# Loading and preparing the first chunk by halves of the heads, under a new fixed order

## The chip, the cores and the metric

The kernel runs on one core of one Trainium2 chip. Its time is the device time of one execution in microseconds (us). The engines are TensorE (PE, matrix products; PEld is its weight load), VectorE (DVE), ScalarE (ACT), GpSimd (POOL) and SyncE (SP), whose queue issues nearly all transfers. 16 DMA engines move the data.

## The reference

There are two stages. The first is a recurrence over 768 steps for 4 batches of 8 heads with head size 40. Each head has a 40x40 state:

```
y[t]  = r[t] @ state                                   (before the update)
Sa    = state @ a[t]
state = state * w[t] - outer(Sa, b[t]) + outer(v[t], k[t])     (w along the columns)
```

The second takes the rows of y (3072 tokens, 320 wide) through `relu(x @ w_in)**2 @ w_out`, with 2048 hidden columns. Inputs and output are 32-bit floats.

## The kernel before

**Chunks.** The recurrence is cut into 12 chunks of 64 steps. In a chunk all 32 heads are worked on together: 16 heads stand in the lower 64 rows of a tile, 16 in the upper. NP is 8, the heads of one batch; the two "halves" h0 and h1 of this text are the first and the second batch in each half of the rows.

**A chunk's preparation** (function `prep`). `ln` takes the logarithm of w on ACT (L453). `hi` is its 16-bit part (L374 where POOL does it) and `lo` the 16-bit remainder (L380 on DVE, L378 on POOL). PE sums both along the steps by a triangular matrix: `ci` by halves of the heads and `cf` for all heads turned. ACT takes exponentials of these sums: `ei` (L475, into iG), `ex` (L481, into Gin), `ef` (L497, into GT). `mulKB` multiplies k and b by iG, by halves; `castA`, `castR`, `castV` bring a, r and v to 16 bits. `TK`, `TA`, `TR` are transposes on PE, and `tK`, `tA`, `tR` take their results out of PSUM. `EN` is a triangle of products, masked by `mEN` (L578).

**The recurrence and its reading** (`rec`, `read`). `AS`, `EV`, `u0`, `NU`, `u1` solve for the chunk's updates, `SC`, `S` and `s` make the next state, `TS` turns it. `TV`, `CX`, `RS` and `Y` give the chunk's rows of y, `XT` turns these for the second stage.

**The second stage** (`ffn`). For each chunk four entries `F` (first 256 rows of w_in) and four `FL` (last 64 rows), `f` (relu, L802 on ACT), `q` (square: L810 POOL, L808 DVE, L812 ACT), and four `O`, the product with w_out; `o` copies it out, `st` stores it. In the last chunk the copy and the store are split in two parts `g0`, `g1`, with `o0`, `st1` on ACT, `o1` on DVE and `st0` on SP.

**The weights** are loaded once, between the first chunks: `lwl` (last rows of w_in), `lwi u0` to `u3` (quarters of w_in, 512 KB each), `lwo x0` to `x7` (pieces of w_out, 320 KB each). They pass through two staging places each, and are cast to 16 bits by `cwl`, `cwi` and `cwo`.

**Loads of the inputs** are `ldw`, `ldk`, `ldb`, `ldv`, `lda`, `ldr`, two DMAs each for one chunk. Two buffers stand for each input, so a load may be issued once the chunk two before it has been used.

**What sets the order.** Each piece of work is an entry ("ACT ln 0", "PE2 TK 0", where the figure is one of four PSUM places). The text ORDER lists all of them, and `issue` emits them in this sequence, so each engine works its entries off strictly in the order of the text. The text is written out in the kernel; it was made by a search outside it, which used the costs given with each entry. Because this order is fixed, the trace's instructions can be matched to the entries one by one on each engine.

On PE an entry works in one of four tilings, given as `mode`: "R" uses 64 rows by 128 columns (ci, cf, EN, CX, FL and all transposes), "Q" 64 by 64 (EV, NU), "C" 128 by 64 (AS, SC, S, RS, Y), "D" 128 by 128 (F, O). The profile writes these as 64*128, 64*64, 128*64 and 128*128.

Of the kernel before, what the change touches and what calls it, by code (L numbers as in the profile page):

```python
# [86 lines left out]
ORDER = """SP ldw 0; SP lda 0; SP ldb 0; SP ldk 0; ACT ln 0; SP ldw 1; POOL hi 0; POOL castA 0; DVE lo 0; PE0  # L87
TA 0; SP lda 1; PE1 ci 0 h0; PE2 ci 0 h1; ACT ex 0 h0 g1; PE3 cf 0; ACT ex 0 h1 g0; ACT ei 0 h1;
ACT ex 0 h1 g1; ACT ei 0 h0; SP ldv 0; ACT ef 0; DVE mulKB 0 h1; SP ldw 2; ACT ex 0 h0 g0; DVE
mulKB 0 h0; DVE tA 0 g0; PE2 TK 0; DVE tK 0; ACT ln 1; SP ldk 1; POOL hi 1; DVE tA 0 g1; PE3 EN 0  # L90
g0; POOL lo 1; DVE mEN 0 g0; PE1 EN 0 g1; DVE mEN 0 g1; SP ldb 1; PE2 ci 1 h1; POOL castV 0 g0;
ACT ei 1 h1; POOL castV 0 g1; ACT ex 1 h1 g1; ACT ex 1 h1 g0; POOL castA 1; PE0 EV 0; SP ldr 1;
PE3 cf 1; ACT u0 0; PE1 ci 1 h0; ACT ln 2; PE NU 0; ACT ex 1 h0 g1; PE2 TA 1; POOL hi 2; ACT ef 1;
SP lda 2; DVE lo 2; ACT u1 0 g0; DVE tA 1 g0; ACT ei 1 h0; SP ldv 1; PE3 S 0 g0; DVE tA 1 g1; ACT
ex 1 h0 g0; ACT u1 0 g1; PE1 ci 2 h0; SP ldr 0; ACT ex 2 h0 g1; PE S 0 g1; DVE mulKB 1 h0; PE2 TV
0; DVE mulKB 1 h1; ACT ei 2 h0; DVE s 0 q1; ACT tV 0; SP ldw 3; PE0 TK 1; DVE s 0 q0; SP ldk 2;
DVE tK 1; PE3 TS 0; ACT tS 0; PE2 EN 1 g1; PE0 cf 2; DVE mEN 1 g1; SP ldb 2; PE3 EN 1 g0; ACT ef
2; POOL castR 0; DVE mEN 1 g0; ACT ex 2 h0 g0; POOL castV 1 g1; ACT castA 2; PE2 TR 0; PE0 ci 2
h1; POOL castV 1 g0; ACT tR 0 g0; PE1 AS 1; SP lwl 0; ACT tR 0 g1; POOL castR 1; PE EV 1; ACT ln
3; PE3 CX 0 g0; PE2 CX 0 g1; ACT u0 1; POOL hi 3; DVE mCX 0 g0; ACT ex 2 h1 g1; PE NU 1; POOL lo  # L100
3; ACT ex 2 h1 g0; SP lwi 0 u0; ACT ei 2 h1; DVE mCX 0 g1; PE3 TR 1; ACT u1 1 g0; PE0 TA 2; ACT tR
1 g1; DVE tA 2 g1; PE2 Y 0; SP ldv 2; ACT tR 1 g0; ACT u1 1 g1; PE3 SC 1; DVE mulKB 2 h1; PE1 TV
1; SP ldr 2; PE S 1 g0; DVE tA 2 g0; ACT tV 1; PE S 1 g1; DVE y 0; DVE mulKB 2 h0; ACT cwl 0; DVE
yd 0; PE0 TK 2; DVE s 1 q0; PE1 ci 3 h1; POOL cwi 0 u0; SP lwi 0 u1; PE2 CX 1 g0; DVE tK 2; ACT ei
3 h1; ACT ex 3 h1 g0; ACT ex 3 h1 g1; SP lwo 0 x1; DVE s 1 q1; PE0 cf 3; PE1 EN 2 g0; DVE mCX 1
g0; ACT ef 3; PE3 TS 1; POOL castV 2 g1; SP lwo 0 x0; ACT tS 1; DVE mEN 2 g0; PE0 EN 2 g1; POOL
castR 2; PE2 AS 2; SP ldb 3; POOL castV 2 g0; DVE mEN 2 g1; PE3 ci 3 h0; PE1 XT 0; ACT ex 3 h0 g0;
POOL cwi 0 u1; ACT ei 3 h0; DVE xt 0; PE EV 2; ACT ex 3 h0 g1; SP lwi 0 u3; PE0 CX 1 g1; ACT u0 2;
PE1 FL 0 u1; DVE mCX 1 g1; PE NU 2; SP lda 3; PE3 RS 1; ACT u1 2 g0; PE0 SC 2; PE Y 1; DVE u1 2
g1; SP ldk 3; PE F 0 u1; DVE y 1; SP lwi 0 u2; DVE yd 1; PE S 2 g0; ACT f 0 u1; PE S 2 g1; PE2 TR  # L110
2; DVE s 2 q0; PE3 FL 0 u3; ACT tR 2 g1; POOL cwi 0 u3; DVE s 2 q1; ACT tR 2 g0; SP ldw 4; DVE q 0
u1; POOL castA 3; PE F 0 u3; POOL cwo 0 x0; PE1 TV 2; ACT f 0 u3; DVE cwo 0 x1; PE2 XT 1; PE0 TS
2; SP lwo 0 x2; ACT tV 2; PE3 F 0 u0; DVE tS 2; POOL mulKB 3 h0; DVE xt 1; PE0 TA 3; PE FL 0 u0;
SP lwo 0 x3; DVE tA 3 g1; PE2 FL 1 u3; ACT f 0 u0; PE1 CX 2 g0; POOL cwi 0 u2; DVE tA 3 g0; PE F 1
u3; SP ldv 3; DVE mulKB 3 h1; PE3 F 1 u2; ACT f 1 u3; DVE mCX 2 g0; SP ldr 3; PE0 TK 3; ACT ln 4;
PE FL 1 u2; PE2 FL 1 u1; DVE tK 3; PE1 CX 2 g1; ACT f 1 u2; POOL hi 4; PE F 1 u1; POOL cwo 0 x2;
DVE mCX 2 g1; PE3 F 1 u0; POOL lo 4; ACT cwo 0 x3; PE0 EN 3 g0; ACT f 1 u1; SP lwo 0 x5; PE FL 1
u0; DVE mEN 3 g0; PE1 F 0 u2; ACT f 1 u0; SP lwo 0 x4; PE FL 0 u2; DVE q 0 u0; PE2 EN 3 g1; POOL
castV 3 g0; PE0 cf 4; ACT f 0 u2; DVE mEN 3 g1; PE3 ci 4 h0; SP ldw 5; POOL castV 3 g1; ACT ef 4;
PE1 RS 2; DVE q 0 u2; PE Y 2; ACT ei 4 h0; PE2 AS 3; DVE yd 2; PE EV 3; DVE cwo 0 x5; ACT ex 4 h0  # L120
g1; DVE y 2; PE0 O 0 u0; SP lwo 0 x7; ACT u0 3; POOL cwo 0 x4; DVE q 1 u0; ACT ex 4 h0 g0; POOL
castR 3; ACT q 0 u3; PE1 ci 4 h1; SP lwo 0 x6; PE NU 3; ACT ex 4 h1 g1; PE3 TR 3; ACT u1 3 g0; SP
ldk 4; PE O 0 u1; DVE tR 3 g1; ACT ex 4 h1 g0; DVE u1 3 g1; ACT ei 4 h1; PE O 0 u2; POOL cwo 0 x7;
SP ldb 4; ACT tR 3 g0; ACT ln 5; PE1 XT 2; DVE cwo 0 x6; PE2 TV 3; SP lda 4; POOL hi 5; DVE xt 2;
PE3 SC 3; ACT tV 3; PE S 3 g0; POOL lo 5; PE S 3 g1; PE O 0 u3; DVE s 3 q1; SP ldv 4; DVE s 3 q0;
POOL q 1 u1; PE1 ci 5 h0; ACT o 0; PE2 CX 3 g0; SP ldk 5; PE3 cf 5; ACT ex 5 h0 g0; DVE mCX 3 g0;
# [831 lines left out]
```

## Time and profile before

| | us |
|---|---|
| median of 3 runs | 255.05 |
| lowest, highest run | 252.43, 256.12 |
| profiled execution | 251.61 |
| its span, first to last instruction | 249.8 |
| PE busy in the span | 219.0 (88%) |
| DVE busy | 181.7 (73%) |
| ACT busy | 172.7 (69%) |
| POOL busy | 117.9 (47%) |
| DMA, share of 16 engines, loads and stores of SP | 66.1% |

Busy times are averages over stretches that differ. A row of a group or of the timeline names the line of the kernel, the engine, the operation, and what it writes from what; in square brackets stands the idle time of the engine just before it and what ended that. The line is often that of a helper (L384 is every matmul, L388 every transpose, L374 every cast on POOL), so the tiles tell which entry it is: `pb<-XT,WIN` is F, `pb<-XT,WLAST` is FL, `pb<-WOUT,G` is O, `WIN<-G` is cwi, and `G<-in_moe_w_in_dram` is lwi or lwl.

### The profile page before, as it was taken

What the parts mean: (1) busy time and instruction counts of PE and PEld (TensorE: products, weight loads), DVE (VectorE), ACT (ScalarE), POOL (GpSimd) and SP (SyncE); (2) the same over time, 40 slices, a digit from 0 to 9 for tenths busy, and PEclk for the clock granted to TensorE, in tenths of its full rate; (3) what the DMA queues carried; (4) which work ended last, traced back from release to release, by engine and by line L of the source; (5) the groups of instructions that cost most, each with busy time, mean ns of one, the idle gap of its engine ahead of it and who ended that gap; (6) DMA issues with size and microseconds to landing.
All of it is one profiled execution on the core that took longest, in us unless ns stands there. A gap on an engine that the chain in (4) does not pass through costs nothing.

```text
span 249.8 us, 12572 instructions
## 1 busy us (share of the span) xinstructions
PE 219.0 (88%) x5752; PEld 170.7 (68%) x5752; DVE 181.7 (73%) x227; ACT 172.7 (69%) x231; POOL 117.9 (47%) x119
## 2 busy tenths in 40 slices
PE   0458877777999999999999999999999999999991
PEld 0336765565777777787778778877777777877770
DVE  7585869768787897867868958788778899746221
ACT  2548897756897866788659788895798351863930
POOL 4261341534636587473487870625369930452000
PEclk9999997999999999999999999999999999999998
DMA  6999889999988987878877888976480020201121
GB/s 132 170 150 211 156 172 204 230 228 187 188 213 157 158 209 150 172 167 163 165 178 134 142 136 209 158 169 127 110 140 5 4 58 5 55 3 29 26 55 52
DMA packets 114091, 33.58 MB, mean 134 GB/s; under 512 B 101238, under 2 KB 113014, under 8 KB 114038
## 3 DMA queue, kind: packets, MB, share of 16 engines
q1 hardware_dynamic: 113894, 32.62, 66.1%
q8 instruction: 45, 0.74, 1.3%
q10 hardware_dynamic: 144, 0.16, 0.2%
q14 instruction: 8, 0.07, 0.1%
HBM read 28.84 MB, written 3.93 MB: 131 GB/s over the span
## 4 chain that ended last, share of the span: by engine, by line
PE 61%; ACT 14%; issue 7%; DVE 7%; POOL 6%; DMA 3%; SPq 1%; POOLq 0%; ACTq 0%
PE pb L384 52%; PE pb L388 8%; ACT Gin L481 2%; POOL G L810 2%; ACT iG L475 2%; DMA raw_a<-in_a_dram 2%; DMA raw_w<-in_w_dram 2%; ACT G L802 2%; DVE EN L578 2%; ACT GT L497 2%; ACT VUT L370 1%; DVE KBT L365 1%; DVE AR L365 1%; ACT AR L370 1%; ACT osb L370 1%
## 5 line engine op out<-in xcount | busy, mean ns | idle before, releaser
L802 ACT ACTIVATE G<-pb 128x1024 bf16<-128x1024 f32 x44 | 44.6, 1021 | 19.5 <-PE pb L384 17.4
L384 PE MATMUL pb<-WOUT,G 128*128 128x320 bf16 x384 | 57.3, 300 | 0.0
L810 POOL TENSOR_TENSOR G<-G 128x1024 bf16<-128x1024 bf16 x21 | 41.1, 1966 | 23.3 <-ACT G L802 23.2
L384 PE MATMUL pb<-XT,WIN 128*128 128x256 bf16 x384 | 48.5, 273 | 1.3 <-POOL WIN L374 1.3
L384 PEld LDWEIGHTS <-G 128*128 128x128 bf16 x384 | 35.3, 98 | 14.8 <-issue 1.4
L384 PEld LDWEIGHTS <-WIN 128*128 128x128 bf16 x384 | 34.9, 98 | 8.9 <-issue 2.5
L578 DVE TENSOR_TENSOR CX<-pb,MSKI 128x1024 bf16<-128x1024 f32 x24 | 29.1, 1221 | 7.3 <-PE pb L384 7.0
L578 DVE TENSOR_TENSOR EN<-pb,MSK 128x1024 bf16<-128x1024 f32 x24 | 28.9, 1221 | 6.7 <-PE pb L384 6.4
L481 ACT ACTIVATE Gin<-pb 64x320 f32<-64x320 f32 x48 | 20.6, 429 | 10.3 <-PE pb L384 9.7
L374 POOL CAST VU<-raw_v 64x640 bf16<-64x640 f32 x24 | 17.8, 742 | 12.7 <-DMA raw_v<-in_v_dram 12.1
L670 DVE TENSOR_TENSOR STb<-pb,GT 64x640 bf16<-64x640 f32 x22 | 18.0, 820 | 3.6 <-PE pb L384 3.1
L370 ACT ACTIVATE osb<-pb 128x640 f32<-128x640 f32 (+1 forms) x13 | 8.3, 640 | 17.4 <-PE pb L384 17.0
L374 POOL CAST hi<-lnW 128x640 bf16<-128x640 f32 x12 | 9.2, 767 | 21.9 <-ACT lnW L453 16.9
L475 ACT ACTIVATE iG<-pb 128x640 f32<-128x640 f32 x24 | 16.7, 696 | 3.8 <-PE pb L384 3.6
L384 PEld LDWEIGHTS <-EN 64*64 64x64 bf16 x768 | 15.0, 113 | 6.2 <-issue 3.6
L380 DVE TENSOR_TENSOR KB<-raw_kb,iG 128x640 bf16<-128x640 f32 x16 | 14.4, 914 | 6.7 <-DMA raw_kb<-in_b_dram 4.1
L553 DVE TENSOR_TENSOR AR<-pb,GT 128x512 bf16<-128x512 bf16 x24 | 15.8, 684 | 2.2 <-PE pb L388 2.0
L384 PE MATMUL pb<-XT,WLAST 64*128 64x256 bf16 x192 | 17.2, 271 | 0.1
L808 DVE TENSOR_TENSOR G<-G 128x1024 bf16<-128x1024 bf16 x13 | 11.0, 850 | 8.4 <-ACT G L802 8.4
L378 POOL TENSOR_TENSOR KB<-raw_kb,iG 128x640 bf16<-128x640 f32 x8 | 12.6, 1583 | 8.3 <-ACT iG L475 4.1
L370 ACT ACTIVATE VUT<-pb 128x2048 bf16<-128x2048 bf16 x8 | 15.0, 1873 | 2.2 <-PE pb L388 2.2
L365 DVE COPY KBT<-pb 128x2048 bf16<-128x2048 bf16 x11 | 13.4, 1220 | 3.5 <-PE pb L388 3.5
(82 smaller groups left out, 414.9 us busy)
## 6 DMA issues: line engine op xcount, KB each, us to landing
raw_w<-in_w_dram SPq DMA_DIRECT2D x24, 160.0 KB
raw_a<-in_a_dram SPq DMA_DIRECT2D x24, 160.0 KB
raw_kb<-in_b_dram SPq DMA_DIRECT2D x24, 160.0 KB
raw_kb<-in_k_dram SPq DMA_DIRECT2D x24, 160.0 KB
raw_v<-in_v_dram SPq DMA_DIRECT2D x24, 160.0 KB
raw_r<-in_r_dram SPq DMA_DIRECT2D x22, 160.0 KB
out_dram<-osb SPq DMA_DIRECT2D x22, 160.0 KB
osb<-in_moe_w_out_dram SPq DMA_DIRECT2D x8, 320.0 KB
```

The lines of the kernel that those rows point to most:

```text
L365: lambda: nc.vector.tensor_copy(out=o_(), in_=i_())))
L370: alts.append(("ACT", c_act(n), lambda: nc.scalar.activation(out=o_(), in_=i_(), func=ACTF.Copy, scale=1.0 if scale is None else scale)))
L374: lambda: nc.gpsimd.tensor_copy(out=o_(), in_=i_())))
L384: return lambda: nc.tensor.matmul(out=o_(), lhsT=l_(), rhs=r_(), start=start, stop=stop, skip_group_check=True)
L388: return lambda: nc.tensor.transpose(out=o_(), in_=i_(), identity=IDb[rows(g), :])
L475: ew(f"ei {c} h{jh}", [("ACT", c_act(2 * n), lambda hb=hb, jh=jh: nc.scalar.activation(out=iG[0][:].rearrange("p (g j) e -> p g (j e)", g= ...
L481: nc.scalar.activation(out=Gin[c % NGI][rows(g), NP * jh:NP * jh + NP, :].rearrange("p j e -> p (j e)"), in_=slot(hb, FP32)[rows(g), g, 0: ...
L553: ew(f"tA {c} g{g}", [("DVE", c_dve(512), lambda g=g: nc.vector.tensor_tensor(out=steps(AR[q2][:, 0, g]), in0=turned(ha, g), in1=steps(GT[ ...
L578: evac(f"m{nm} {c} g{g}", lambda s, n: [("DVE", c_dve(n), lambda: nc.vector.tensor_tensor(out=dst[q2][:, g, s].rearrange("p q i t -> p (q ...
L670: ew(f"s {c} q{q}", [("DVE", c_dve(2 * n), lambda q=q: nc.vector.tensor_tensor(out=STb[q2][rows(q), :, q, 0:D], in0=slot(hs, FP32)[rows(q) ...
L802: ("ACT", c_act(1024), lambda gb=gb, hf=hf: nc.scalar.activation(out=gb, in_=slot(hf, FP32)[:], func=ACTF.Relu)),
L810: ("POOL", 1900, lambda gv=gv: nc.gpsimd.tensor_tensor(out=gv, in0=gv, in1=gv, op=ALU.mult)),
```

## The change

For chunk 0 alone, three loads and three steps of the preparation become two entries each, one for each half of the heads:

- `ldw 0`, `ldk 0`, `ldb 0` become `h0` and `h1`, of two DMAs each; a DMA now brings one batch (8 heads, 80 KB) instead of two.
- `ln 0`, `hi 0`, `lo 0` become `h0` and `h1`, on 320 columns instead of 640.
- `ci 0 h0` waits for `hi` and `lo` of its own half alone, and `mulKB 0 h0` for its own half of k and b. `cf 0` waits for both halves.

For the other chunks nothing is split. The text ORDER is replaced as a whole: for all 12 chunks the sequence on each engine, the engine of many elementwise entries and the PSUM place of many products are others than before.

```
+    def parts(c):
+        return [(f" h{j}", (j,)) for j in range(2)] if c == 0 else [("", (0, 1))]
...
+        def quarter(x, g, j):
+            return x[2 * g + j, :, t0, :].rearrange("h t e -> t h e")
...
+            def go(x=x, ring=ring, js=(0, 1)):
+                for g in range(2):
+                    if len(js) == 2:
+                        nc.sync.dma_start(out=ring[c % len(ring)][rows(g)], in_=half(x, g))
+                    else:
+                        nc.sync.dma_start(out=ring[c % len(ring)][rows(g), NP * js[0]:NP * js[0] + NP],
+                                          in_=quarter(x, g, js[0]))
+            for sfx, js in parts(c):
+                plan.add(f"ld{nm} {c}{sfx}", [("SP", 1200 * len(js))],
+                         ("ew", {"SP": lambda go=go, js=js: go(js=js)}),
+                         writes=[("raw", nm, c % len(ring), j) for j in js])
...
-        ew(f"ln {c}", [("ACT", c_act(640), lambda: nc.scalar.activation(
-            out=lw[:], in_=raw_w[c % NW][:], func=ACTF.Ln))],
-           reads=[("raw", "w", c % NW)], writes=[("lnW",)])
...
+        for sfx, js in parts(c):
+            j0, nj = NP * js[0], NP * len(js)
+            def js_(x, j0=j0, nj=nj):
+                return x[:, j0:j0 + nj]
+            ew(f"ln {c}{sfx}", [("ACT", c_act(D * nj), lambda js_=js_: nc.scalar.activation(
+                out=js_(lw), in_=js_(raw_w[c % NW]), func=ACTF.Ln))],
+               reads=[("raw", "w", c % NW, j) for j in js], writes=[("lnW", j) for j in js])
...
-            pe(f"ci {c} h{jh}", "R", n, ms, reads=[("hi",), ("lo",)], writes=[hb], alloc=[hb])
+            pe(f"ci {c} h{jh}", "R", n, ms, reads=[("hi", jh), ("lo", jh)], writes=[hb], alloc=[hb])
```

The loads of SP, in order, up to the last piece of w_out:

```
before: ldw 0; lda 0; ldb 0; ldk 0; ldw 1; lda 1; ldv 0; ldw 2; ldk 1; ldb 1; ldr 1; lda 2; ldv 1;
  ldr 0; ldw 3; ldk 2; ldb 2; lwl 0; lwi 0 u0; ldv 2; ldr 2; lwi 0 u1; lwo 0 x1; lwo 0 x0; ldb 3;
  lwi 0 u3; lda 3; ldk 3; lwi 0 u2; ldw 4; lwo 0 x2; lwo 0 x3; ldv 3; ldr 3; lwo 0 x5; lwo 0 x4;
  ldw 5; lwo 0 x7; lwo 0 x6
after: ldw 0 h1; ldw 0 h0; ldk 0 h0; ldk 0 h1; ldb 0 h0; ldb 0 h1; ldw 1; lda 0; ldv 0; ldw 2;
  lda 1; ldk 1; ldb 1; ldr 0; lwi 0 u0; ldr 1; ldv 1; lda 2; ldk 2; ldb 2; ldw 3; ldr 2; lwl 0;
  lda 3; ldv 2; lwo 0 x1; lwi 0 u1; ldb 3; lwo 0 x3; lwi 0 u3; ldk 3; lwo 0 x0; lwi 0 u2; ldw 4;
  ldr 3; lwo 0 x2; lda 4; ldv 3; lwo 0 x5; lwo 0 x4; ldw 5; lda 5; lwo 0 x7; lwo 0 x6
```

The first entries of the other engines after the change, and the last of ACT:

```
ACT   ln 0 h1; ln 0 h0; ei 0 h1; ef 0; ex 0 h1 g0; ei 0 h0; ex 0 h0 g1; ex 0 h0 g0; ln 1; ...
POOL  hi 0 h1; hi 0 h0; lo 0 h1; lo 0 h0; mulKB 0 h1; castA 0; lo 1; castV 0 g1; castV 0 g0; ...
DVE   mulKB 0 h0; hi 1; tK 0; tA 0 g0; tA 0 g1; mEN 0 g0; mEN 0 g1; tA 1 g1; ...
PE    ci 0 h1; ci 0 h0; cf 0; TK 0; TA 0; EN 0 g0; cf 1; EN 0 g1; ci 1 h0; ci 1 h1; EV 0; ...
ACT   ... o 10; o0 11 g0; st1 11 g0; o0 11 g1; st1 11 g1     (before: o0 g0; o0 g1; st1 g0; st1 g1)
```

More of the change, by code (lines that the diff above doesn't have):

```diff
@@ L98 @@
[L98 to L103, printed above, removed]
@@ L110 @@
[L110 to L115, printed above, removed]
@@ L122 @@
[L122 to L126, printed above, removed]
-PE0 FL 2 u1; ACT ef 5; PE F 2 u1; DVE mulKB 4 h0; ACT ex 5 h0 g1; PE2 F 2 u2; ACT f 2 u1; SP ldb
```

279 lines of the change are left out of this document (151 added, 128 removed).

## The prediction

> **What bounds the kernel now.** I read the engines' busy times by stretches first, then the timeline at the places where TensorE (PE) stands, then the queue that issues the loads (SPq). Columns of the first view: stretch, PE busy (matmuls), weight loads, DVE, ACT, POOL, granted clock, DMA share, GB/s.
>
> ```profile
> 0.00:20.00 20.00, 7.14 (x180) 5.46 (x182) 13.71 (x28) 8.66 (x14) 8.11 (x22) 1.00 1.02 152
> 20.00:40.00 20.00, 16.61 (x532) 13.45 (x528) 14.88 (x19) 17.48 (x27) 5.65 (x7) 0.92 0.92 190
> 40.00:60.00 20.00, 14.62 (x514) 11.89 (x515) 15.20 (x20) 14.07 (x18) 8.10 (x9) 1.00 1.01 206
> 60.00:80.00 20.00, 18.09 (x459) 13.56 (x458) 15.04 (x20) 15.93 (x23) 11.29 (x13) 1.00 0.88 193
> 80.00:160.00 80.00, 78.52 (x2130) 61.30 (x2125) 63.12 (x74) 61.85 (x85) 49.17 (x44) 1.00 0.83 164
> 160.00:240.00 80.00, 79.59 (x1937) 62.09 (x1934) 57.83 (x67) 53.40 (x67) 35.62 (x26) 1.00 0.30 63
> ```
>
> Two regimes show. Up to 60 us the DMA engines are full (shares 1.02, 0.92, 1.01) and PE is busy 38.4 of 60 us. From 80 us PE is busy 158.1 of 160 us and nothing else matters. The seam is one load, the third quarter of the first weight matrix:
>
> ```profile
> 60.62 1.15 POOL L374 CAST WIN<-G 128x1024 bf16<-128x1024 f32 x1 [0.58 <-DMA G<-in_moe_w_in_dram]
> 61.82 0.39 PE L384 MATMUL pb<-XT,WIN 128*128 128x256 bf16 x2 [1.35 <-POOL WIN L374]
> ```
>
> POOL waits for the DMA, casts, and PE waits 1.35 us for the cast (entry F 1 u2 of the order). Past this point PE hardly waits. So the time is: when F 1 u2 may start, plus PE's own work behind it, plus its waits, plus the tail.
>
> PE's work I take from starts of neighbouring entries. This stretch of its timeline shows how:
>
> ```profile
> 84.06 1.92 PE L384 MATMUL pb<-XT,WIN 128*128 128x256 bf16 x16
> 85.92 0.39 PE L384 MATMUL pb<-XT,WLAST 64*128 64x256 bf16 x4
> 86.15 0.30 PE L384 MATMUL pb<-hi,UTI 64*128 64x320 bf16 x2
> 86.28 0.30 PE L384 MATMUL pb<-lo,UTI 64*128 64x320 bf16 x2
> 86.42 0.40 PE L384 MATMUL pb<-AR,VUT 64*128 64x64 bf16 x16
> 86.75 1.26 PE L384 MATMUL pb<-WOUT,G 128*128 128x320 bf16 x8
> ```
>
> An FL entry (rows 64*128, x4) takes 0.23 us from its start to that of another 64*128 entry (85.92 to 86.15). A CX entry (x16) takes 86.75 - 86.42 = 0.33 where a 128*128 entry follows; the median CX followed by its own kind takes 0.24. The step between tilings thus costs 0.09 us. By the same difference O costs 1.10 and 1.19, F 0.88 and 0.97, FL 0.23 and 0.32, S 0.25 and 0.34: 0.095 us a step. Medians of the unswitched entries in us: F 0.88, O 1.10, FL 0.23, ci 0.28, cf, TK, TV and TS 0.47, EN, CX, TA and TR 0.24, EV and NU 0.52, Y 0.51, RS, SC and AS 0.30, S 0.25, XT 0.18. Summed from F 1 u2 on, the old order has 163.4 us of work and 150 tiling steps (14.2 us): 177.6. From 61.8 this gives 239.4; the last matmul ends at 244.4, so 5.0 us are waits, in small pieces.
>
> **The change, part by part.**
>
> **1. The halves at the start: 0 at the seam.** Each of w, k, b of chunk 0 becomes two entries of two DMAs: 12 issues where 6 were, and the load of a moves behind all of them and the next w.
>
> ```profile
> 0.79 1.46 SPq L400 DMA_DIRECT2D raw_w<-in_w_dram  x2
> 2.30 1.31 SPq L421 DMA_DIRECT2D raw_a<-in_a_dram  x2
> 3.65 1.33 SPq L407 DMA_DIRECT2D raw_kb<-in_b_dram  x2
> 5.83 0.74 ACT L453 ACTIVATE lnW<-raw_w 128x640 f32<-128x640 f32 x1 [3.76 <-DMA raw_w<-in_w_dram]
> ```
>
> An issue takes 0.65 to 0.73 us. Two issues end at 2.25 and the logarithm starts at 5.83, 3.6 us later; the first half cannot save more than its share of the data (160 KB at 152 GB/s: 1.1 us), so ln 0 h1 starts near 4.6. The second half's issues end near 3.4, so its logarithm gains nothing (about 5.7). A half Ln costs some 0.43 (the 64x320 rows of L481), a half cast some 0.4 and a half subtraction on POOL 0.7 (half of 1.45). POOL's queue is hi h1, hi h0, lo h1, lo h0: from 6.1 it ends near 8.0, where DVE's whole lo ended at 8.76. That gains 0.8 us for ci and cf. But it is spent at once: b's last half is issued by 8.7 and lands near 10.5, a is issued 10.0 to 11.3 and lands near 13.2, and POOL has the half product mulKB (1.58) ahead of the cast of a (0.73). TA 0, done at 8.75 before, comes at 14; hi 1 (0.5 to 0.7) now stands before tK 0 on DVE. I get EN 0 at 16.0, against 15.34. Bounds of this edit for the first products: 1 us earlier to 1 us later. The DMA stream, not this chain, sets the seam at 60 us and hides it, so it enters as 0; without that cover it would be the 0.7 us of EN 0.
>
> **2. The stream starts slower: +1.0.** Twelve issues at 0.66 take 7.9 us; their data (80 KB each at 152 GB/s: 0.54 us) take 6.5. So the issuing queue holds the stream back by 1.4, and a full stream doesn't catch up. Bounds: 0 (later queueing absorbs it) to 2. The Trainium skill ("DMA: Bandwidth & Descriptors", Issuing engines are not separate DMA queues) says that the time on the sequencer to initiate a DMA is usually small relative to the DMA itself; by it this term would be 0 and the forecast 1.0 lower. The rows here, 0.66 to issue against 0.54 to move, speak against it for pieces of this size.
>
> **3. The new order of loads: +1.3.** Counted to the load that gates F 1 u2 (lwi 0 u2), both orders hold w, a, k, b of four chunks, v and r of three, the last rows of the first matrix and its four quarters; the new one has three pieces of the second matrix ahead of it instead of two. A piece is 320 KB; at 206 GB/s 1.6 us, and its packets near 61 us ran 1.3. Bounds 0 to 1.6. The cast goes from POOL to DVE; the cast's 640 columns took 0.67 on DVE and 0.72 on POOL, so nothing is gained. F 1 u2 starts at 61.8 + 1.0 + 1.3 = 64.1.
>
> **4. PE's work behind it: +2.0.** The new order holds 164.1 us there and 163 tiling steps (15.5): 179.6 against 177.6. Before it PE has room, so what was moved there costs nothing. In all the new order makes 194 steps, the old 181; the products are the same.
>
> **5. Waits: -1.2.** The other engines gain 2.3 us of lead at the seam; I let a half of that come off the 5.0 us. Bounds -3 to +3: the last piece of the second matrix (lwo 0 x6) now has two more loads of a ahead of it, lands later by 2 to 4 us than its 74.9, and O 0 u3, which started at 78.0, would come near 64.1 + 15.2 = 79.3, so it can wait a microsecond.
>
> **6. Tail: +0.6.** At the end ACT's queue had both copies, then both stores; now a store stands before the second copy.
>
> ```profile
> 245.14 0.30 ACT L370 ACTIVATE osb<-pb 128x160 f32<-128x160 f32 x1 [0.39 <-DVE osb L365]
> 245.15 0.99 ACTq L854 DMA_DIRECT2D out_dram<-osb  x2
> 245.48 0.33 DVE L365 COPY osb<-pb 128x160 f32<-128x160 f32 x1 [0.37 <-ACT osb L370]
> ```
>
> The store's issue on ACT takes 0.3 to 0.63 us; the copy that went beside it, DVE's behind it, and the last stores wait for it. Bounds 0.3 to 0.65.
>
> **Sum**: +1.0 + 1.3 + 2.0 - 1.2 + 0.6 = +3.7 us. The profiled execution took 251.6 (span 249.8 and 1.8 around it), so 255.3 for its like. The median of the runs, 255.05, lies 3.4 above it with the same program; I add 3.7 to the median: **258.7**.
>
> **Rivals.**
> - **The seam comes earlier, not slower than before: 253.9, chance 0.2.** If the third quarter lands before 59.5, F 1 u2 starts at 60.5 (its 1.35 us wait is gone) and half of the 5.0 us of waits with it: 60.5 + 179.6 + 2.5 = 242.6, 1.8 before 244.4; with the tail, -1.2. For it: SPq stood from 45.2 to 48.5 for POOL's cast of an earlier quarter, and the new order spreads these casts over POOL, DVE and ACT. Against: the DMA share was 1.01 in these 20 us all the same.
> - **POOL becomes the bound: 261.7, chance 0.25.** By mean durations its entries go from 117 to 140 us (19 half products mulKB at 1.58 instead of 8, 24 squares at 1.97 instead of 21), ACT's from 181 to 166, DVE's from 184 to 186. POOL was busy 8.6 of 10 us from 140 to 150 and 9.9 from 190 to 200; 22 us more over the 130 us from 60 to 190 is 1.7 per 10. It decides where a transpose TK waits for POOL's mulKB by over 1 us; 3 us in all. DVE's mulKB also took 1.3 instead of 0.82 where POOL worked beside it. Against: POOL idled 23 us for ACT's G, so it has room on average.
> - **The halves shorten nothing because the load of a binds**: that is step 1, and gives the forecast.
>
> **Chances.** Forecast 0.5, the first rival 0.2, POOL 0.25, other mishaps 0.05. Range: the bounds around the forecast give 255 to 262; the first rival widens it down: 253.0 to 262.5. A measurement of this kernel tells about 2%, 5.1 us, from no change (250.0 to 260.2). Faster by over 2%: 0.04; slower by over 2%, most of the POOL case and the forecast's upper end: 0.30; within: 0.66.
>
> **What would show it.** Right: F 1 u2 behind a cast of WIN at 63 to 65 us, the DMA share near 1 until then, PE full from 80 us, some 1.2 us more PE time in steps, 0.6 us more between the last matmul and the end. Wrong: PE gapless already near 60 us (first rival), or PE waits over 0.5 us for KB or a square from POOL behind 80 us (second).

## The result, and the profile after

The changed kernel takes 261.62 us (median of 5 runs, 260.21 to 265.17), the kernel before beside it 254.59 (251.68 to 256.12): a ratio of 1.031, 95% interval 1.025 to 1.037. I had forecast 258.7, 3.7 us more than the median of before; it became some 7 to 8 us, twice as much, inside the range and on the side where I had put 0.30.

Both profiled executions are single ones. That of after (261.62, span 259.9) is the median of its runs, that of before (251.61, span 249.8) lies below the lowest of its own (251.68) and 3.0 us below their median. This matters: b_steps below, which is the program of before for 100 us, starts O 0 u3 3.8 us later in its profile, and b_compute_halves, which differs from before only in three steps at the start, 2.2 us later. The ratios below compare the fast runs of both kernels, and the profiles of a_whole_loads, b_steps, b_x_behind and b_cast_late show executions more than 1.5% above the fastest of their kernel.

The same stretches as in the prediction, in the profile after (stretch, PE busy, weight loads, DVE, ACT, POOL, granted clock, DMA share, GB/s):

```profile
0.00:20.00 20.00, 6.83 (x160) 4.99 (x160) 14.09 (x27) 7.91 (x12) 9.94 (x24) 1.00 0.80 138
20.00:40.00 20.00, 15.95 (x512) 13.28 (x512) 14.31 (x17) 14.46 (x24) 8.33 (x10) 0.91 0.87 169
40.00:60.00 20.00, 14.99 (x452) 12.30 (x450) 15.45 (x21) 9.16 (x12) 6.99 (x8) 0.75 0.93 197
60.00:80.00 20.00, 15.07 (x364) 10.98 (x365) 13.00 (x16) 16.24 (x20) 9.00 (x10) 0.91 0.83 189
80.00:160.00 80.00, 78.42 (x2084) 59.26 (x2080) 62.21 (x73) 56.51 (x82) 50.85 (x43) 1.00 0.85 164
160.00:240.00 80.00, 78.08 (x2080) 61.43 (x2080) 62.33 (x70) 44.39 (x63) 47.86 (x37) 1.00 0.33 70
```

The two regimes have stayed, but the second begins later: from 60 to 80 us PE executes 364 matmuls where it executed 459. The DMA share, which was 1.02 in the first 20 us, is 0.80. The queue of the loads shows why (start, duration, what is issued):

```profile
0.80 2.78 SPq L411 DMA_DIRECT2D raw_w<-in_w_dram  x4
3.62 2.67 SPq L425 DMA_DIRECT2D raw_kb<-in_k_dram  x4
6.33 2.67 SPq L425 DMA_DIRECT2D raw_kb<-in_b_dram  x4
9.04 1.35 SPq L409 DMA_DIRECT2D raw_w<-in_w_dram  x2
```

Twelve issues stand wall to wall, 0.67 to 0.70 us each, and the second chunk's w gets its turn at 9.04 instead of 7.06. The seam of the prediction, in the timeline:

```profile
66.66 0.69 DVE L366 CAST WIN<-G 128x1024 bf16<-128x1024 f32 x1 [2.45 <-DMA G<-in_moe_w_in_dram]
67.41 0.82 PE L385 MATMUL pb<-XT,WIN 128*128 128x256 bf16 x3 [1.20 <-DVE WIN L366]
```

F 1 u2 starts at 67.41, not at 64.1 as forecast (61.82 before). A second place follows that I had only touched on: the last piece of the second weight matrix.

```profile
84.37 0.74 ACT L371 ACTIVATE WOUT<-osb 128x640 bf16<-128x640 f32 x1
84.68 0.63 PE L389 MATMUL pb<-IDb,VU 64*128 64x64 bf16 x32
85.24 1.26 PE L385 MATMUL pb<-WOUT,G 128*128 128x320 bf16 x8
```

O 0 u3 starts at 85.24 (78.04 before), 0.13 us behind that cast. PE comes straight from TV 3 and has no idle time in front of it, so in the changed kernel the last piece is not yet a wait; it becomes one as soon as PE gets there earlier. From there PE runs to its last matmul in 169.3 us (before 166.4), 2.0 of the 2.9 us being work and tiling steps. The chain of work that ended last names the loads: beside PE's 58% of it stand SP's queue with 13% and DMA with 10%; before these were 1% and 3%, and ACT had 14%. A part of it in order of time (start, duration, what):

```profile
44.26 2.89 SPq L917
...
47.32 5.93 DMA G<-in_moe_w_in_dram
...
53.28 0.70 DVE WIN L366
...
55.79 4.80 SPq L917
...
60.63 6.01 DMA G<-in_moe_w_in_dram
```

L917 issues a piece of the second weight matrix (lwo), into one of two staging places (osb). For 2.89 and 4.80 us SP stands at the issues of x1 and x0, and the quarters of the first matrix that PE waits for are queued behind them. It does not stand for staging there: x1 and x0 are the first pieces in their two places. Each of the two issues ends while three earlier loads are still in flight, that of x0 at 60.59, 0.3 us before lwi 0 u3 lands. A load whose buffer has long been free can stand as long. Here are x0 and then ldr 3 in the changed kernel, whose buffer was free from 31.2 on and whose first DMA takes 3.04 us to issue, and ldr 2 in the kernel before (free from 29.8 on, 3.20 us):

```profile
55.79 4.80 SPq L917 DMA_DIRECT2D osb<-in_moe_w_out_dram  x1
63.30 3.68 SPq L450 DMA_DIRECT2D raw_r<-in_r_dram  x2
```

```profile
37.45 3.84 SPq L431 DMA_DIRECT2D raw_r<-in_r_dram  x2
```

The profile names nothing that these issues wait for. That it is the loads ahead of them in the queue is read from the times at which those land. (Here and below a load lands with the last increment of its semaphore in the trace, which is what its users wait for; the expectations count its last packet, 0.3 to 1.4 us earlier.) Staging holds SP at another place: x3 is issued at 50.94, 1.4 us after the load ahead of it, when the cast of x1 has ended.

All landmarks at a glance, each from the profile of the kernel named (us from the start of the span; the last column is the tail):

| | EV 0 | F 1 u2 | O 0 u3 | last matmul ends | to the end of the span |
|---|---|---|---|---|---|
| before | 17.27 | 61.82 | 78.04 | 244.41 | 5.4 |
| after | 20.16 | 67.41 | 85.24 | 254.54 | 5.4 |

### The profile page after: what moved, and what is told of

Read it like the earlier page. It is cut to its first block, busy times and chain, and to the rows that moved or that the text cites. A ratio compares the mean times of both kernels' runs of the same rounds, so it can differ in the third digit from the quotient of the medians.

```text
span 259.9 us, 12582 instructions
## 1 busy us (share of the span) xinstructions
PE 223.9 (86%) x5752; PEld 173.1 (67%) x5752; DVE 185.8 (71%) x227; ACT 158.0 (61%) x221; POOL 136.8 (53%) x132
## 4 chain that ended last, share of the span: by engine, by line
PE 58%; SPq 13%; DMA 10%; DVE 8%; ACT 4%; POOL 3%; issue 3%; ACTq 0%; POOLq 0%; DVEq 0%
PE pb L385 52%; PE pb L389 6%; DMA G<-in_moe_w_in_dram 5%; SPq L917 3%; POOL G L837 2%; SPq L423 2%; SPq L425 2%; DMA raw_r<-in_r_dram 2%; SPq L440 2%; DMA raw_a<-in_a_dram 2%; DMA raw_w<-in_w_dram 2%; DVE CX L605 1%; DVE EN L605 1%; SPq L409 1%; SPq L411 1%
## 5 line engine op out<-in xcount | busy, mean ns | idle before, releaser
L837 POOL TENSOR_TENSOR G<-G 128x1024 bf16<-128x1024 bf16 x24 | 45.1, 1891 | 34.9 <-ACT G L829 34.9
L385 PE MATMUL pb<-WOUT,G 128*128 128x320 bf16 x384 | 58.0, 300 | 0.2 <-POOL G L837 0.2
L385 PE MATMUL pb<-XT,WIN 128*128 128x256 bf16 x384 | 49.7, 276 | 3.8 <-DVE WIN L366 2.1
L379 POOL TENSOR_TENSOR KB<-raw_kb,iG 128x640 bf16<-128x640 f32 x19 | 29.7, 1569 | 31.7 <-DMA raw_kb<-in_k_dram 16.0
L375 POOL CAST VU<-raw_v 64x640 bf16<-64x640 f32 x23 | 16.7, 730 | 7.5 <-DMA raw_v<-in_v_dram 6.3
L375 POOL CAST tR<-raw_r 128x640 bf16<-128x640 f32 x12 | 8.6, 719 | 19.5 <-DMA raw_r<-in_r_dram 13.8
L839 ACT ACTIVATE G<-G 128x1024 bf16<-128x1024 bf16 x14 | 14.7, 1053 | 4.1 <-DVE G L831 4.1
L379 POOL TENSOR_TENSOR lo<-lnW,hi 128x640 bf16<-128x640 f32 (+1 forms) x13 | 16.9, 1305 | 0.6
L524 ACT ACTIVATE GT<-pb 128x1024 f32<-128x1024 f32 x12 | 12.2, 1016 | 5.9 <-PE pb L385 5.9
L767 DVE TENSOR_TENSOR Yb<-pb,Gin 128x640 bf16<-128x640 f32 (+1 forms) x24 | 12.4, 551 | 4.7 <-PE pb L385 4.7
```

The costliest lines, as they stand in the source:

```text
L375: lambda: nc.gpsimd.tensor_copy(out=o_(), in_=i_())))
L379: return [("POOL", 40 + 2.35 * n, lambda: nc.gpsimd.tensor_tensor(out=o_(), in0=a_(), in1=b_(), op=op)), ("DVE", c_dve(n), lambda: nc.vect ...
L385: return lambda: nc.tensor.matmul(out=o_(), lhsT=l_(), rhs=r_(), start=start, stop=stop, skip_group_check=True)
L837: ("POOL", 1900, lambda gv=gv: nc.gpsimd.tensor_tensor(out=gv, in0=gv, in1=gv, op=ALU.mult)),
L839: ("ACT", c_act(1024), lambda gv=gv: nc.scalar.activation(out=gv, in_=gv, func=ACTF.Square))],
```

## The experiments

Each ratio stands against runs of the kernel before on the same chip in the same session (medians there 252.5 to 254.9). Where two kernels of different sessions are compared, it is by these ratios.

### The parts of the change alone

**b_halves**: the order of before, with each of ldw 0, ldk 0, ldb 0, ln 0, hi 0 and lo 0 replaced by its two halves in place.

```
-SP ldw 0;           ... -ACT ln 0;           -POOL hi 0; -DVE lo 0;
+SP ldw 0 h0; ldw 0 h1 ... +ACT ln 0 h0; ln 0 h1 +POOL hi 0 h0; hi 0 h1 +DVE lo 0 h0; lo 0 h1
```

> The old order with the halves alone: w, k, b of chunk 0 loaded by halves, logarithm, hi and lo by halves on the engines that had them, everything else as before. Theory S: 12 issues hold the stream back by 1.4 to 2.1 us, F 1 u2 starts at 63.2 to 63.9 instead of 61.8, the time rises by 1.4 to 2.1 over that of before (1.0055 to 1.008). Rival H (the halves do what they say, an earlier start): F 1 u2 at 61.0, 0.8 us faster than before. Rival O: no change.

Measured: 258.09 us median of 10, ratio 1.015 (1.010 to 1.021). That is 3.9 us, nearly twice the upper end of what was expected; the rival of an earlier start is refuted. In its profile cf 1 starts at 21.91, 2.54 later than before's, and this shift stays to within 0.1 us through NU 0, S 0, EV 1 and S 1 up to 40 us. cf 1 stands behind EV 0 on PE, and EV 0 waits 1.6 us for a cast of the first v, which landed at 20.16 instead of 16.29.

**b_compute_halves**: the same without the halved loads; only the logarithm, hi and lo are made by halves.

```
-            for sfx, js in parts(c):          # of the loads
+            for sfx, js in [("", (0, 1))]:
```

> The order of before, first w, k and b loaded whole as there, only the logarithm and its two parts made by halves (three more instructions at the start; b_halves without the halved loads). Theory S (the halves cost through six more DMAs on SP ahead of ldw 1, cf 1 starting 2.5 us later): cf 1 starts at 19.2 to 20.0, within 0.6 of before's 19.36, and the time is 254 to 256, as before. Rival C (the halved compute costs by itself, hi and lo of both halves standing one behind the other on POOL and DVE): ci 0 h0 and cf 0 a microsecond later and the time at 256 to 258, like b_halves.

Measured: 255.47, ratio 1.002 (0.997 to 1.008); cf 1 at 19.20. The halved arithmetic costs nothing that the interval shows; the halved loads are what costs. It is the times that show this: at F 1 u2 the profiles of the two kernels lie 0.1 us apart (64.63 and 64.54). Six more issues delay the landing of ldw 1 from 13.19 to 15.26 us. The first stretches, before and then b_halves, show the DMA engines underfed rather than full (columns as above):

```profile
0.00:5.00 5.00, 0.00 (x0) 0.00 (x0) 3.77 (x16) 1.28 (x1) 2.52 (x15) 1.00 0.54 108
5.00:10.00 5.00, 1.86 (x38) 1.39 (x40) 3.42 (x6) 1.31 (x3) 1.38 (x2) 1.00 1.30 180
10.00:15.00 5.00, 1.70 (x58) 1.38 (x52) 3.29 (x4) 3.97 (x7) 0.82 (x2) 1.00 1.29 178
```

```profile
0.00:5.00 5.00, 0.00 (x0) 0.00 (x0) 3.76 (x16) 1.42 (x2) 2.53 (x15) 1.00 0.37 60
5.00:10.00 5.00, 1.60 (x30) 1.13 (x32) 3.70 (x7) 1.22 (x3) 1.62 (x3) 1.00 0.77 150
10.00:15.00 5.00, 1.17 (x44) 1.01 (x42) 1.86 (x3) 3.40 (x7) 0.00 (x0) 1.00 0.93 170
```

By the last column, 466 x 5 = 2330 KB against 380 x 5 = 1900 KB in the first 15 us: 430 KB, or 2.4 us of before's 178 GB/s, close to the shift of cf 1.

**a_order_only**: the changed kernel with the halves undone in loads and arithmetic; the new order alone.

> The changed kernel's order with the halves undone altogether: first w, k, b loaded whole and their logarithm, high and low part made whole, as in before. This is the new order alone. Theory A (the two parts add up: halves some 1.5%, the new order the rest): 257 to 259.5, some 1.6% above before. Rival M (the new order's second seam takes back what the whole loads gain at the first, as the profile of a_whole_loads showed, 2.0 us at F 1 u2 and 0.8 at O 0 u3): 260 to 262, as the changed kernel.

Measured: 259.63, ratio 1.025 (1.020 to 1.031), between the two theories: 2.5% above before where A expected 1.6. The new order alone is thus the larger part of the loss, about 6 us; undoing the halves in it is worth 2.4 us at F 1 u2 (65.01) and 3.6 at O 0 u3 (81.62) in the profile, but the intervals of the times, 1.020 to 1.031 and 1.025 to 1.037, overlap.

### What could give the halves' loss back

**b_halves_k_act**: b_halves with the four quarters of the first k issued by ACT's queue.

```
+                q = nc.scalar if nm == "k" and c == 0 else nc.sync
-                        nc.sync.dma_start(out=to[:, ...], in_=quarter(x, g, js[0]))
+                        q.dma_start(out=to[:, ...], in_=quarter(x, g, js[0]))
```

> The order of before with the halves of the change, and the four quarter loads of the first k handed out by ACT's queue instead of SP's; nothing else differs from the kernel b_halves (258.09 us, F 1 u2 at 64.6, the last matmul ending at 250.5). Theory S (the halves cost because SP hands out its first DMAs wall to wall at some 0.68 us each, so that six more of them push the whole stream of loads): four issues less on SP give back 2.7 us: ldw 1 lands by 11.7, F 1 u2 starts at 61.9 to 62.6, the last matmul ends at 247.5 to 248.5, the time is 255 to 256. Rival D (it is not the issue but the transfers themselves: twice as many, smaller transfers keep the queues busy, whoever hands them out): ldw 1 lands at 14 as before, F 1 u2 stays at 64 to 65, the time at 258.

Measured: 257.14, ratio 1.013 (1.006 to 1.021), not told apart from b_halves. ldw 1 lands at 13.58, 1.7 earlier than in b_halves (so far theory S), but w and a of the first chunk land later (6.83 and 8.64 instead of 6.56 and 7.46), TA 0 starts 1.1 later, and of the 2.5 us at cf 1 only 1.2 come back. F 1 u2 is at 65.62, outside theory S's 61.9 to 62.6.

**b_kb_act**: the kernel before, with the first k and b, whole, on ACT's queue.

> The kernel before, with the first k and b (whole, as there) handed out by ACT's queue, which has nothing to do until the first w has landed; no halves, no new order. Theory S: four issues less ahead of ldw 1 on SP bring the stream 2.7 us ahead at most: ldw 1 lands at 9.0 to 9.5 instead of 11.8, F 1 u2 starts at 59.5 to 61, the time is 252 to 253.5 (1 to 2 us less; the start's own chain on PE, TA 0 to NU 0, cannot gain the whole). Rival D (the transfers themselves bound the start): nothing moves, 254 to 255.

Measured: 255.14, ratio 1.005 (1.001 to 1.010): no gain, rather a small loss. Its two queues, in the timeline:

```profile
0.80 1.74 SPq L400 DMA_DIRECT2D raw_w<-in_w_dram  x2
0.84 1.44 ACTq L408 DMA_DIRECT2D raw_kb<-in_k_dram  x2
2.30 2.75 ACTq L408 DMA_DIRECT2D raw_kb<-in_b_dram  x2
2.58 1.88 SPq L422 DMA_DIRECT2D raw_a<-in_a_dram  x2
...
7.62 0.74 ACT L454 ACTIVATE lnW<-raw_w 128x640 f32<-128x640 f32 x1 [5.53 <-DMA raw_w<-in_w_dram]
```

The first four issues on SP now take 0.60 to 1.24 us instead of 0.60 to 0.76, and w, which everything waits for, shares the engines with k and b: ln 0 starts at 7.62 instead of 5.83, TA 0 and the chain behind it, to cf 1 and S 0, 2.56 us later. That speaks for rival D, though it had expected no loss: with whole loads the transfers bound the start, and with halves the issues, which stand wall to wall.

The two runs also part the chain from the stream. cf 1 is 2.5 us late in both, which costs 0.5% here and 1.5% in b_halves (the intervals touch at 1.010). The loads are late in b_halves alone: ldb 1 lands at 22.85 in before, 22.37 here and 26.04 there. The Trainium skill (DMA: Bandwidth & Descriptors, section "Issuing engines are not separate DMA queues") says that DMAs of all issuing engines interleave on the same 16 engines, and that issuing from several saves only sequencer time, usually small beside the DMA. Its first half agrees with b_kb_act; its "usually small" does not hold for the quarter loads, 0.67 us of issue for 80 KB, whose data take some 0.54 us by the prediction's estimate.

### The first place: what is ahead of lwi 0 u2

**a_whole_loads**: the changed kernel with the first w, k and b loaded whole.

> The new order, with w, k and b of chunk 0 loaded whole again (6 issues instead of 12); logarithm, hi and lo stay in halves. Theory S (the seam: the stream of loads, held back by the issuing queue at the start, sets when F 1 u2 may start, and what it loses there is lost at the end): F 1 u2 starts 2 us earlier (65.4 instead of 67.4) and the time falls by 2, from 261.6 to 259.6. Rival O (the loss lies in the new order behind the seam, in TensorE's tiling steps and POOL's work, and the seam's lateness is absorbed by waits): no change, 261.6.

Measured: 261.13, 261.26, 261.38 and once 256.77; no ratio is on record, and neither theory is told from the other by these times. F 1 u2 at 65.39, as expected; but O 0 u3 at 84.40 and the last matmul at 254.2. Of 2.0 us gained at the first place 0.8 are left at the second and 0.3 at the end.

**a_x0_behind** (SP's lwo 0 x0 behind lwi 0 u2 instead of ahead of it) and **a_x0_x3** (x0 in the place of x3, x3 behind lwi 0 u2):

> The new order, with one piece of the second weight matrix (lwo 0 x0) issued behind the load that gates F 1 u2 instead of ahead of it. Theory S: F 1 u2 starts 1.6 us earlier (65.8), the time falls by 1.6 to 260.0. Rival O: no change, 261.6.

> The new order, with lwo 0 x0 in the place of lwo 0 x3 and lwo 0 x3 behind the load that gates F 1 u2: one piece fewer ahead, and the issuing queue no longer stands for the cast that frees x3's staging place (1.4 us between 49.5 and 50.9). Theory S: F 1 u2 starts 3.0 us earlier (64.4), the time falls to 258.6. Rival O: no change, 261.6. If only the piece counts and not the standing queue: 260.0, as in the run with lwo 0 x0 moved alone.

Measured: 261.82, ratio 1.027 (1.016 to 1.037), and 260.78, ratio 1.020 (1.010 to 1.031). In both F 1 u2 starts at 63.98, 3.4 us before the changed kernel's, and the lead grows to 4.7 us by EV 3; then O 0 u3 waits 1.0 and 2.1 us for the last piece and 3.7 and 2.6 us are left. Not all of the 3.4 us is the piece's own. From the landing of lwi 0 u3 to that of lwi 0 u2 it takes 4.5 to 6.2 us in the four profiles with x0 between them (after, where it is 5.7, a_casts, a_whole_loads and a_order_only) and 3.2 to 4.5 in the five without a piece there (3.8 and 3.9 in these two): by the means of 5.6 and 3.9 the piece costs 1.7 us. Of the 4.6 us by which lwi 0 u2 lands earlier in a_x0_behind than in after, 2.6 are there already at lwi 0 u3, which is handed out ahead of x0 in both. The times do not show any of it beyond their spread.

### The second place: the last pieces

In the changed kernel ACT makes four of the casts of the second matrix, in its fixed order among the second stage's activations. x3 lands at 55.53 and is cast at 68.4; x2 lands at 70.60 and is cast at 73.6 to 74.3, and x4, which needs x2's staging, cannot be issued before. The loads behind it wait with it. SP's queue shows the standing (4.01 us for the issues of x5 and x4, 2.6 of them between the two):

```profile
68.88 1.69 SPq L433 DMA_DIRECT2D raw_v<-in_v_dram  x2
70.68 4.01 SPq L917 DMA_DIRECT2D osb<-in_moe_w_out_dram  x2
74.74 1.32 SPq L409 DMA_DIRECT2D raw_w<-in_w_dram  x2
```

**a_casts** moves six casts in the order:

```
-ACT  cwo 0 x3; cwo 0 x2; cwo 0 x5; cwo 0 x6
+POOL cwo 0 x3 behind castV 2 g1; x2 behind castR 3; x5 and x4 behind castV 3 g1; x6 behind castA 4
-DVE  cwo 0 x7 behind u1 3 g0
+DVE  cwo 0 x7 behind y 2
```

> The changed kernel with six casts of the second weight matrix made at other places: x2, x3, x5 and x6 on POOL instead of ACT, x4 earlier on POOL and x7 earlier on DVE; loads and PE's order are the same. Theory T (a second seam: the last pieces' loads wait for staging that ACT's casts hold, and O 0 u3 waits for the last cast): F 1 u2 stays at 67.4, lwo x5 no longer waits, the last cast is done by 81, and O 0 u3 starts at 82.6 to 83.6 in place of 85.2; the last matmul ends at 252 to 253, the time is 259 to 260.5. Rival P (behind F 1 u2 PE's own work and the chain through it set the pace): O 0 u3 stays within 0.6 of 85.2 and the time at 261 to 262.

**a_all** adds the whole loads and lwo x0 behind lwi u2:

> The changed kernel's order with the first w, k and b loaded whole (the compute still by halves), lwo x0 handed out behind lwi u2, and the casts of a_casts. If the two seams S and T are what the new order loses beyond its PE work, both go: F 1 u2 at 61.5 to 62.5, O 0 u3 at 77.7 to 79, the last matmul at 247 to 248.5, the time 254 to 256, which is before plus the 2.0 us of further steps on PE and what is left in waits. Rival P (the new order's own chain): F 1 u2 gains as in the single runs, but O 0 u3 stays above 81 and the time above 258.

Measured: 264.52, ratio 1.042 (1.036 to 1.049), and 266.19, ratio 1.048 (1.041 to 1.055): both slower than before by more than the changed kernel is. In a_casts both theories missed. In a_all rival P's figures hold (O 0 u3 at 85.30), but what holds O 0 u3 up is the new place of two casts. Up to O 0 u0 they gain as meant, 2.7 and 4.9 us. Then this, on DVE in a_casts:

```profile
80.54 0.49 DVE L366 CAST WOUT<-osb 128x640 bf16<-128x640 f32 x1 [3.01 <-DMA osb<-in_moe_w_out_dram]
80.94 0.82 DVE L368 TENSOR_SCALAR NZ<-pb 128x640 bf16<-128x640 f32 x1
```

The cast of x7 stands at the head of DVE's queue for 3.01 us, and u0 3 (NZ), which NU 3 on PE waits for, stands behind it; POOL waits likewise for x6, 3.75 us, with the squaring q 0 u2 behind. The waits that I took from SP I had put at the head of engines which PE needs. What theory T took for a wait in the changed kernel, the last cast in front of O 0 u3, was none there, as the row of TV 3 above shows.

**a_all2**: a_all with x7 and x6 cast where the changed kernel casts them (and x2 behind lo 4).

> As a_all (first w, k, b loaded whole, lwo x0 behind lwi u2), but only the casts x3, x2, x5 and x4 are moved; x7 and x6 are cast where the changed kernel casts them, since in a_casts and a_all x7 on DVE stood ahead of u0 3 and waited for its load, and NU 3 behind it lost 2.9 us. Up to EV 3 it should be where a_all was (74.9, 4.9 us ahead of the changed kernel). Theory T (what was left behind F 1 u2 was the last pieces' staging): NU 3 at 76.5 to 77.5, O 0 u3 at 80 to 81.2, the last matmul at 249.5 to 251, the time 256 to 258. Rival P (another wait of the new order takes the place): O 0 u3 above 82, the time above 259.

Measured: 259.59, ratio 1.022 (1.015 to 1.030). F 1 u2 starts at 61.12, before that of before itself, EV 3 at 71.89 and NU 3 at 73.69, 7.9 us ahead of the changed kernel, more than expected. O 0 u3 is at 79.70, 0.3 earlier than theory T had it, and yet there PE waits for the last piece:

```profile
78.92 0.74 ACT L371 ACTIVATE WOUT<-osb 128x640 bf16<-128x640 f32 x1 [2.08 <-DMA osb<-in_moe_w_out_dram]
79.70 1.95 PE L385 MATMUL pb<-WOUT,G 128*128 128x320 bf16 x8 [2.30 <-ACT WOUT L371]
```

Of the 7.9 us 5.5 are left at O 0 u3, 4.0 at O 1 u3, and 3.5 at the last matmul (251.06). The time misses the expected 256 to 258, and the ratio's interval overlaps that of the changed kernel (1.025 to 1.037).

**a_all3**: a_all2 with ldw 5 and lda 5 issued behind lwo x7 and x6.

> a_all2 with ldw 5 and lda 5 handed out behind lwo x7 and x6 instead of ahead of them; in a_all2 O 0 u3 waited 2.4 us for x6 (landed at 78.3). Theory T: x6 lands by 75.5, O 0 u3 starts at 77.3 to 78.2 instead of 79.7, the last matmul ends at 248.5 to 250, the time is 257 to 258.5; what is then left to before is the 2 us of PE's further work and steps and 1 us of waits. Rival Q (the loads displaced, ldw 5 and lda 5, become late in turn): O 0 u3 gains but O 1 u3 does not, time 259 to 260.

Measured: 261.27, ratio 1.031 (1.024 to 1.037). x6 did not land by 75.5 but at 78.50, and O 0 u3 is at 82.20. The displaced loads became late, as rival Q had it, but at once: O 0 u3 does not gain, it loses 2.5 us against a_all2.

```profile
79.93 0.74 ACT L477 ACTIVATE lnW<-raw_w 128x640 f32<-128x640 f32 x1 [3.81 <-DMA raw_w<-in_w_dram]
80.69 0.70 ACT L371 ACTIVATE VU<-pb 64x640 bf16<-64x640 f32 x1
81.41 0.74 ACT L371 ACTIVATE WOUT<-osb 128x640 bf16<-128x640 f32 x1
```

The logarithm of the sixth chunk now waits 3.81 us for its own displaced load, and the cast of x6 stands behind it.

### The price of a change of tiling

**b_steps**: the kernel before, 21 pairs of neighbours in PE's order exchanged (CX 4 g1 and O 2 u3, TA 6 and RS 4, EN 6 g0 and SC 5, ...), so that PE changes its tiling 215 times instead of 181.

> The kernel before with 21 pairs of neighbours in PE's order exchanged between 104 and 230 us, each pair's second with its inputs ready 2 us or more earlier; PE changes its tiling 215 times instead of 181, everything else is the same. By the price of 0.095 us for one change the last matmul ends 3.2 us later from O 0 u3 on (169.6 instead of 166.4 us behind it), waits of the exchanged pairs add 0 to 1, and the time is 257 to 259. Rival N (a change of tiling costs nothing, the 0.095 is another effect of the kind of matmul): the distance stays at 166 to 167.4 and the time at 254 to 255.5.

Measured: 263.69, ratio 1.036 (1.026 to 1.045), 5 us above the expected time. The starts of neighbouring entries behind 85 us, taken apart as in the prediction (start to start, less the entry's own work):

| | changes of tiling | median each | all others | sum of excesses over 0.4 us |
|---|---|---|---|---|
| before | 130 | 0.095 us | 0.000 us | 1.6 us |
| b_steps | 167 | 0.096 us | 0.000 us | 8.7 us |
| after | 148 | 0.094 us | 0.000 us | 3.7 us |

The price holds: excesses under 0.4 us at changes add up to 16.4 us instead of 13.1, 3.3 more as expected, and rival N is refuted. The rest are waits of the exchanged pairs. I had looked at their inputs only, not at PSUM: TS 9, for one, was moved ahead of F 9 u0 and now waits 1.5 us until CX 10 g0 has been read out of its slot.

### The same place in the kernel before

b_steps and before are one program for 100 us, and their profiles agree to 0.04 us up to 39 us; then F 0 u3 starts at 58.87 against 54.54, F 1 u2 at 64.02 against 61.82, O 0 u3 at 81.84 against 78.04. b_compute_halves shows the same (58.08, 64.54, 80.25), so it is the profile of before that is early here. Two causes meet there in b_steps: EV 2 waits 2.1 us for castV 2 g0 (47.8 to 48.5), which stands on POOL behind the casts of lwi 0 u0 and of r (castR 2 at 47.0, landed at 46.96), and F 0 u3 waits 2.0 us for lwi 0 u3.

**b_x_behind** (lwo x1 and x0 behind lwi 0 u2), **b_cast_late** (cwi 0 u0 behind castV 2 g0 on POOL) and **b_x_cast** (both):

```
SP:   lwi 0 u1; -lwo 0 x1; -lwo 0 x0; ldb 3; lwi 0 u3; lda 3; ldk 3; lwi 0 u2; +lwo 0 x1; +lwo 0 x0; ldw 4
POOL: -cwi 0 u0; castV 2 g1; castR 2; castV 2 g0; +cwi 0 u0; cwi 0 u1
```

> The kernel before with lwo x1 and x0 handed out behind lwi u2 instead of ahead of lwi u3, and their casts moved behind cwi u2 on POOL and behind tA 3 g0 on DVE. There F 0 u1, F 0 u3 and F 1 u2 waited 1.5 us and less for lwi u1, u3 and u2. Theory W (weight pieces in the order in which PE uses them take these waits away): lwi u3 and u2 land 2 us earlier, F 1 u2 starts at 60 to 61.2 instead of 61.8, the time is 253 to 254 (0.5 to 1.5 less). Rival E (the chain of the first chunks' compute sets F 1 u2 as much as the weights do, as the equal shifts of all starts in the runs so far show): F 1 u2 gains less than 0.5, and O 0 u0 may wait for x0: 254.5 to 256.

> The kernel before with the cast cwi u0 behind castV 2 g1, castR 2 and castV 2 g0 on POOL instead of ahead of them. In the executions of before's own first 100 us that b_steps and b_compute_halves show, cwi u0 waited on POOL for lwi u0 until 43.3 to 43.7, and EV 2 behind castV 2 g0 waited 1.6 to 2.1 us. Theory V (POOL's order there costs): EV 2 starts at 46.5 to 47.2, F 1 u2 at 61.8 to 63, time 252.5 to 254. Rival W (the weight stream sets F 0 u3 and F 1 u2 whatever the chain does): EV 2 gains, F 0 u3 still waits for lwi u3, F 1 u2 at 63.5 to 64.5, time 254 to 255.5.

> The kernel before with both edits, that of b_x_behind (lwo x1 and x0 behind lwi u2) and that of b_cast_late (cwi u0 behind the casts of the third chunk's v and r on POOL). In b_cast_late EV 2 gained but F 0 u3 waited 4.0 us for lwi u3 (landed at 56.5); in b_x_behind lwi u3 landed at 52.6 but EV 2 and F 0 u1 came 2.7 and 3.6 us late. Theory B (two holds at one place, and the time only moves when both go): F 0 u1 at 51.5 to 53, F 0 u3 at 54.5 to 56 without a wait over 1 us, F 1 u2 at 61 to 62.5, time 251.5 to 253.5. Rival L (the last pieces, which now land later, take it back at O 0 u3: x6 landed at 81.1 in b_x_behind): F 1 u2 gains, O 0 u3 stays at 81 to 82, time 254 to 256.

Measured: b_x_behind 257.01, ratio 1.010 (1.005 to 1.015), above both its theories, with F 1 u2 at 65.12; b_cast_late 254.74, ratio 0.995 (0.990 to 1.000); b_x_cast 254.45 where before took 252.49, ratio 1.010 (1.004 to 1.017). b_cast_late is rival W in the profile: EV 2 at 47.45 (48.57 in b_steps), but then F 0 u3 waits for its weights,

```profile
57.45 1.04 POOL L374 CAST WIN<-G 128x1024 bf16<-128x1024 f32 x1 [7.50 <-DMA G<-in_moe_w_in_dram]
58.55 1.89 PE L384 MATMUL pb<-XT,WIN 128*128 128x256 bf16 x8 [3.95 <-POOL WIN L374]
```

and F 1 u2 is at 65.83. b_x_cast takes both away: F 0 u3 at 54.80 and F 1 u2 at 60.53, better than theory B's range and the earliest of all kernels here. And it is lost again within ten microseconds. x0, now behind, is cast at 62.6 to 63.3; SP issues x2 and x3 only then, x3 lands at 68.70, and ACT waits for it with the stage's activations behind:

```profile
68.72 0.74 ACT L370 ACTIVATE WOUT<-osb 128x640 bf16<-128x640 f32 x1 [3.46 <-DMA osb<-in_moe_w_out_dram]
69.37 2.83 ACT L802 ACTIVATE G<-pb 128x1024 bf16<-128x1024 f32 x3
```

EV 3 starts at 74.31 and O 0 u3 at 81.88, as in b_steps. That is rival L, though its wait came earlier than at O 0 u3, and its place is ACT's queue.

No kernel here is surely faster than before: the interval of b_cast_late ends at 1.000.

## Why the prediction was wrong

**The frame held.** The time is the start of the stretch that PE fills, plus PE's work, its waits and the tail. The terms of it were mis-sized. Between the two profiles the last matmul moves by 10.1 us: 5.6 at F 1 u2 (forecast 2.3), 2.0 of PE's work (2.0), 2.5 of waits (-1.2); the tail adds 0 (0.6). About 3 of the 10.1 us are not the change's, since the profile of before is that much below the median of its runs. By ratio, the halves alone cost 3.9 us where steps 1 and 2 gave 1.0, and the order alone 6.4 where steps 3 to 6 gave 2.7.

**Step 1 (the halves at the start, 0 at the seam)** held for the arithmetic (b_compute_halves 1.002). In the changed kernel EN 0 g0 came at 17.28, later than my 16.0 and than the "1 us later" of its bounds: the load of a landed at 14.99, not near 13.2. That the stream and not this chain sets the seam is borne out in part: b_kb_act has the chain late by 2.5 us and loses 0.5%.

**Step 2 (the stream starts slower, +1.0, bounds 0 to 2)** is the first that failed, by its size. I set 7.9 us of issuing against 6.5 of data, and then took 1.0 where that gives 1.4. But the six issues push back every load behind them: in b_halves ldw 1 lands 2.1 us later, ldb 1 3.2, and cf 1 starts 2.5 later. In time it is 1.5% or 3.9 us in the old order. In the new order it is 2.0 (a_whole_loads) to 2.4 us (a_order_only) at F 1 u2, and 0.6% in time, not told from none.

**Step 3 (one more piece ahead of lwi 0 u2, +1.3)** was nearer than the two profiles make it look. They have 5.6 us at F 1 u2 (67.41 against 61.82) where steps 2 and 3 gave 2.3. The piece itself comes to 1.7 us by the landings; the base was early, since F 1 u2 is at 64.02 to 65.83 in the other profiles of the old order but b_x_cast; and lwi 0 u3 landed 6.9 us behind its issue in after, where three other profiles with the new order's loads have 5.0 to 5.4 (a_x0_behind, a_x0_x3, a_whole_loads). One reading of rows was wrong: I took the cast's 0.67 on DVE from a piece of 640 columns and found no gain. The cast of 1024 columns took 0.69 on DVE where POOL took 1.15.

**Step 4 (PE's work, +2.0)** held. From O 0 u3 on the model has 164.4 us of work and steps in the new order and 162.4 in the old; b_steps confirms the price of a step.

**Step 5 (waits, -1.2)** failed in sign. PE's waits from F 1 u2 on are 254.54 - 67.41 - 179.6 = 7.5 us, not 3.8; I had let the other engines' lead pay for some of them. In a_order_only they are 6.7 us, and in no profile of the new order fewer, where before has 5.0 (up to 9.1 in other profiles of the old order). Up to O 0 u3 the changed kernel has 2.7 us of them and before 1.0. None stands at O 0 u3 itself, of which I had written that it "can wait a microsecond" for the last piece, and which I had left out of the sum. It waits only where PE comes earlier: 1.0 us in a_x0_behind, 2.1 in a_x0_x3, 2.3 in a_all2. So what a better first place gains is in part lost there, and moving the casts only moved the wait (a_casts, a_all2, a_all3). Of the waits behind O 0 u3 some belong to the new order itself: in the profiles of after, a_order_only, a_all2 and a_all3 cf 11 stands 1.4 us each time until DVE has taken CX 9 g0 out of its slot:

```profile
211.18 0.21 PE L385 MATMUL pb<-UTI,hi 64*128 64x64 bf16 x2 [1.41 <-DVE CX L605]
```

**Step 6 (tail, +0.6)**: from the last matmul to the last issue the copies and stores take 2.4 us instead of 1.7, as forecast, but what follows is 0.7 us shorter; 5.4 us before and after. It came out at 0.

**The rivals.** The earlier seam did not come. POOL is busy 136.8 us (140 forecast, 117.9 before), but behind 80 us PE waits for POOL nowhere by more than 0.5 us; that its forecast time, 261.7, is close to the result is luck. I had no case for an engine whose queue is held up by a load.

By ratio the halves alone cost 3.9 us and the order alone 6.4, together 10.3 where the change costs 8.0; the intervals leave room for a plain sum. What stays open is where the order's 6.4 us lie, beyond the 2.0 of PE's work. The profile of a_order_only (258.47) is 7.0 us longer than that of before, 3.6 of it up to O 0 u3 and 3.3 behind it. But O 0 u3 is at 78.0 to 82.3 in six profiles of the old order without halves, and before's is the earliest by 3.7 us. One profile of each does not tell how the 6.4 us divide in the mean of many runs.
